# A long convolution rebuilt inside a two-phase kernel: phases by matmul, amplitudes by exponential, a 32x2 by 32 spectral split

## Chip, cores and metric

One core of a Trainium2 chip. The metric is device time in microseconds of one execution, the median of repeated runs. Engines are named as in the profile: PE (TensorE, matmul) and PEld (its weight loads), DVE (VectorE), ACT (ScalarE), POOL (GpSimd), SP (SyncE, here only a DMA queue).

## The reference, cut to what matters

Everything is float32, with L = 2048 positions, D = 512 channels, N = 128 modes per channel, F = 1792.

```python
x = A_u                                   # [1, 2048, 512]
h = x + conv(layernorm(x))
h2 = h + mixer(layernorm(h))

# conv
dt = exp(log_dt); A = -exp(log_A_real) + 1j*A_imag; C = (C_real + 1j*C_imag)*dt[:, None]
P = exp((A*dt[:, None])[:, :, None] * arange(L))        # [512, 128, 2048]
K = 2*einsum("dn,dnl->dl", C, P).real                   # the taps, [512, 2048]
y = irfft(rfft(u, 2L) * rfft(K, 2L))[:L] + u*D_skip     # along time, per channel

# mixer
h = gelu(layernorm(x) @ w1); four column groups shifted in time by +1, -1, +2, -2
x1 = x + shifted @ w2
out = x1 + gelu(layernorm(x1) @ w3) @ w4
```

Two parts are costly in the convolution: building the taps K, a sum of 128 damped oscillations for each channel and time, and the convolution itself, done by discrete Fourier transforms written as matmuls.

## The kernel before, in words

`tile_kernel` runs `conv_phase` and then `mixer_phase`. The residual `h` stays on chip, 16 blocks of 512 channels on 128 partitions.

**Taps.** Time l is split into a slow and a fast part, so that a tap is a product of two small tables summed over the modes. The modes lie on the 128 partitions. Channels go in 32 chunks of 16 (`CH`). For each chunk `table(g)` builds `cs` and `sn`, [128, 16 x 96] each: 64 columns per channel for one time factor (a lower half of 32 and an upper half of 32) and 32 for the other. A table entry is amplitude times cosine or sine of a phase. Phases are 32-bit integers that wrap once a turn: `params(t)` makes steps and starts for 128 channels, `steps` expands them on POOL into `p8` and `s8`, and `phases` adds them into `pt` on POOL, 1024 integers per partition and chunk. ACT takes sine of `pt` and, after an absolute value, cosine. Amplitudes are products of powers of the decay: `decay` makes powers in `E` by squaring on ACT, DVE multiplies them into the PSUM tile `amx` (in some chunks ACT squares part of them), and `amy` takes the second factor. Then DVE and POOL multiply: `snx` and `csx` on DVE (four operations of 512), `sny` and `csy` on one of the two by `SHARE`. `taps(s, g)` multiplies the tables on PE and ACT copies the result to `kt`.

**Spectra.** Channels go in four stages of 128 (`WID`). A transform of 32 times 64 points: `stage_a_taps` or `stage_a_turn` transforms `kt` over the first index with 32x32 tiles, and either ACT copies or DVE turns the result into `at`; `stage_a_x` does the same with the input. `stage_b` and `product` do the second index with `tbs` (128 rows, 64 columns a tile, eight products per `e`, eight `e` per stage), ACT copies one spectrum, DVE (or POOL, by `SHARE`) multiplies, and `stage_b_inv` goes back with `ms` (64 rows, 128 columns). `stage_a_inv` and `last_a_inv` finish with `fis` and add to `h`. There are two buffers `u` between product and inverse.

**Order.** Nearly every operation of `conv_phase` is a node of a planner (class `Plan`): engine, assumed cost, tiles that it reads and writes, and a nominal due time from `NOM`. The planner walks a model of the engines, the queues, the port that DVE and POOL share and the free PSUM banks (`grab`), and so fixes one order for each engine; `InOrder` then keeps it. Where PE would idle it inserts multiplications by the identity (`busy`). While stage s is transformed, the tables of stage s+1 are built, so the last stage has no tables beside it. PSUM has two banks' pairs, two single banks and `amx`. DMAs go out on the SP queue, except the first blocks of x on ACT's queue.

**Mixer.** Layers of split-precision (fp32r) matmuls on PE with GELU on ACT. It begins when the last quarter of `h` is there: statistics, normalisation (`norm_h`, `norm1`), `warm`, `layer1`.

All engine calls go through one recording helper, so nearly every instruction of the profile bears L88; rows are told apart by tile names.

Of the kernel before, what the change touches and what calls it, by code (L numbers as in the profile page):

```python
# [24 lines left out]
SHARE = {'mul0': [[1, 4], [0, 7]], 'mul2': [[6], []], 'amy': [[0, 1, 2, 3, 5, 6], [0, 1, 3, 4, 5, 6]], 'csy': [[5, 7], [0, 1, 2, 3, 4, 5, 7]], 'sny': [[1, 2, 4, 6, 7], [0, 1, 2, 4, 5, 6, 7]], 'sq': [[0, 1, 2, 3, 7], [1, 2, 3, 4, 6, 7]], 'turn': [[0, 1, 2, 4, 5, 6], [0, 2, 4, 6, 7]], 'hadd': [[0, 2, 6, 7], [1, 5, 6]], 'sum0': [[1, 5], [2, 4, 5]], 'sum1': [[], [2, 7]], 'sum2': [[2, 4, 6, 7], [1, 2, 4, 6, 7]], 'sum3': [[2, 3, 4, 5, 6, 7], [0, 2, 7]]}  # L25
# [8 lines left out]
PAIRS = 2  # L34
# [4 lines left out]
NOM = {'t0': 988.68, 'per': 120.18, 'ln': -591.43, 'kg0': -1777.07, 'kgs0': -98.74, 'kg': 84.04, 'kgs': 113.27, 'ak': 132.4, 'ax': -1187.75, 'b': -2.11, 'ib': 2.35, 'y': 1372.79, 'ys': 271.67, 'tr': -1417.89, 'exp': -7.85, 'wt': 1053.36, 'pr1': -308.92, 'pr2': 976.97, 'st': 1676.95, 'xa': 510.71, 'xs': -31.11}  # L39
TURN = 2.0 ** 32  # L40
TWO_PI = 2.0 * math.pi
SIN_SCALE = float(np.nextafter(np.float32(TWO_PI), np.float32(0))) / TURN
RAD = 683565248.0
# [3 lines left out]
def tables():  # L47
# [5 lines left out]
    a, b, k1, k2 = np.arange(32.0), np.arange(64.0), np.arange(32.0), np.arange(64.0)  # L53
    ph = 2 * np.pi * np.outer(a, k1 + 0.25) / 32
    fa = np.tile(np.stack([np.cos(ph), -np.sin(ph)], 1), (4, 1, 1)).astype(np.float32)
    fi = np.zeros((128, 2, 32), np.float32)
    for hi in range(2):
        fi[hi * 64 : hi * 64 + 64, hi] = np.concatenate([np.cos(ph), -np.sin(ph)], 1).T / L
    th = 2 * np.pi * b[:, None, None] * (k1[None, :, None] + 32 * k2[None, None, :] + 0.25) / L
    tb = np.zeros((128, 32, 128), np.float32)  # L60
    mm = np.zeros((128, 3, 16, 128), np.float32)
    for hi in range(2):
        c, s = np.cos(th[hi * 32 : hi * 32 + 32]), np.sin(th[hi * 32 : hi * 32 + 32])
        r, i = slice(hi * 64, hi * 64 + 32), slice(hi * 64 + 32, hi * 64 + 64)
        q = slice(hi * 32, hi * 32 + 32)
        tb[:64][q, :, :64], tb[:64][q, :, 64:] = c, -s
        tb[64:][q, :, :64], tb[64:][q, :, 64:] = s, c
# [1496 lines left out]
```

## Time and profile before

| | |
|---|---|
| runs | 723.45, 723.99, 725.02 us; median 723.99 |
| profiled execution, span | 723.0 us, 16573 instructions |
| PE busy / PEld | 672.0 us (93%) / 520.1 us (72%) |
| DVE | 536.4 us (74%) |
| ACT | 416.8 us (58%) |
| POOL | 394.9 us (55%) |
| first matmul of the mixer's warm-up | 321.66 us |
| mean granted PE clock | 0.983 |

The convolution fills the first 321.7 us, the mixer the rest. Busy shares over the span are means over these two; the windows by stage in the prediction tell them apart. PE's busy time holds identity multiplications that compute nothing.

### The profile page before, as it was taken

To read this page: it belongs to the slowest core of one execution; us is meant where nothing else is said; L and a number is where in the kernel's file an instruction comes from. 1 tells how busy PE (TensorE), PEld (TensorE's weight loads), DVE (VectorE), ACT (ScalarE), POOL (GpSimd) and SP (SyncE) were. 2 spreads that over 40 slices of the span, in tenths; PEclk is the share of its full clock that TensorE was granted. 3 is DMA by queue.
4 is the path that set the end of the run, shared out by engine and by line. 5 is a ranking of instruction groups with operands and counts; after the bars stand their busy time and mean duration, and the time that the engine had idled before them with its cause. 6 is when DMAs were issued, how large, how long until landed. Compare 5 with 4: busy or idle time off the path is not lost.

```text
span 723.0 us, 16573 instructions
## 1 busy us (share of the span) xinstructions
PE 672.0 (93%) x6812; PEld 520.1 (72%) x6812; DVE 536.4 (74%) x947; ACT 416.8 (58%) x724; POOL 394.9 (55%) x386
## 2 busy tenths in 40 slices
PE   3898499999999989989999999999999999999997
PEld 2887255754762765858888777888888888888886
DVE  3999999999789888988454789754667955545544
ACT  3897778866995887215646344575344644443430
POOL 0687389977997998302344334554345655534310
PEclk9999799999999999999999999999999999999999
DMA  8830053012000213020010002211111152111014
GB/s 229 231 129 16 2 161 76 2 47 77 16 17 24 39 38 98 2 60 0 1 30 29 1 0 59 59 44 44 48 40 60 51 159 81 45 44 58 1 30 117
DMA packets 42667, 40.98 MB, mean 57 GB/s; under 512 B 4704, under 2 KB 31328, under 8 KB 42592
## 3 DMA queue, kind: packets, MB, share of 16 engines
q1 hardware_dynamic: 41440, 37.83, 18.3%
q10 hardware_dynamic: 1152, 2.10, 1.2%
q8 instruction: 53, 0.87, 0.5%
q14 instruction: 22, 0.18, 0.1%
HBM read 33.62 MB, written 6.29 MB: 55 GB/s over the span
## 4 chain that ended last, share of the span: by engine, by line
PE 55%; DVE 21%; ACT 10%; POOL 7%; issue 4%; DMA 2%; SPq 1%; DVEq 0%; ACTq 0%; POOLq 0%
PE l L88 20%; PE acc L88 11%; ACT pt L88 6%; PE bank L88 6%; DVE u L88 4%; DVE at L88 3%; PE l3c L88 3%; PE l3d L88 2%; PE l3f L88 2%; PE l3g L88 2%; PE l3e L88 2%; PE l3a L88 2%; PE l3b L88 2%; DVE bs L88 2%; DVE cs L88 2%
## 5 line engine op out<-in xcount | busy, mean ns | idle before, releaser
L88 ACT ACTIVATE pt<-pt 128x1056 f32<-128x1056 int32 x64 | 70.0, 1094 | 20.6 <-DVE cs L88 8.6
L88 POOL TENSOR_TENSOR pt<-p,s 128x1024 int32<-128x1024 int32 x32 | 65.1, 2039 | 6.2 <-DVE sn L88 5.3
L88 PE MATMUL bank<-at,tbs 128*64 128x256 f32 (+1 forms) x640 | 63.3, 343 | 2.5 <-DVE at L88 1.2
L88 PE MATMUL bank<-ident 128*128 128x128 f32 x472 | 62.8, 288 | 0.0
L88 PEld LDWEIGHTS bank<-ident 128*128 128x128 f32 x472 | 58.0, 200 | 5.7 <-ACT E L88 1.7
L88 PEld LDWEIGHTS bank<-at,tbs 128*64 128x64 f32 x640 | 39.4, 135 | 22.4 <-DVE at L88 3.5
L88 PE MATMUL bank<-u,ms 64*128 64x128 f32 x736 | 50.9, 284 | 4.3 <-DVE u L88 1.8
L88 PEld LDWEIGHTS bank<-u,ms 64*128 64x128 f32 x736 | 44.5, 189 | 12.5 <-issue 4.6
L88 POOL TENSOR_TENSOR cs0w<-raw,cs0w 128x512 fp32r<-128x512 f32 x7 | 9.1, 1302 | 67.0 <-ACT cs0w L88 58.3
L88 DVE TENSOR_TENSOR cs<-pt,amx 128x512 f32<-128x512 f32 x64 | 41.0, 679 | 5.1 <-ACT amx L88 4.4
L88 DVE TENSOR_TENSOR h<-h,l 128x512 f32<-128x512 f32 x48 | 32.6, 686 | 14.9 <-PE l L88 14.8
L88 DVE TENSOR_TENSOR u<-u,l3f 128x512 f32<-128x512 f32 x14 | 9.6, 684 | 44.9 <-PE l3f L88 44.9
L88 POOL TENSOR_TENSOR cs1w<-raw,cs1w 128x512 fp32r<-128x512 f32 x7 | 9.1, 1298 | 61.4 <-ACT cs1w L88 61.4
L88 PE MATMUL bank<-cs 128*32 128x64 f32 x1024 | 32.9, 225 | 8.8 <-DVE cs L88 8.2
L88 PEld LDWEIGHTS bank<-cs 128*32 128x32 f32 x1024 | 24.1, 111 | 20.1 <-issue 14.8
L88 ACT ACTIVATE pt<-pt,halfpi 128x1056 f32<-128x1056 f32 x32 | 38.0, 1189 | 0.4
L88 DVE STREAM_TRANSPOSE at<-bank 128x512 f32<-128x512 f32 (+1 forms) x40 | 36.3, 933 | 1.6 <-PE bank L88 1.3
L88 ACT COPY at<-bank 128x512 f32<-128x512 f32 x40 | 25.2, 632 | 21.2 <-PE bank L88 21.1
L88 POOL TENSOR_TENSOR sn<-pt,amp 128x512 f32<-128x512 f32 x26 | 32.5, 1250 | 7.3 <-DVE amp L88 4.0
L88 ACT ACTIVATE u<-u 128x512 f32<-128x512 f32 x56 | 35.4, 633 | 1.8
L88 POOL TENSOR_TENSOR h<-h,x 128x512 f32<-128x512 f32 x16 | 22.0, 1384 | 24.7 <-DVE x L88 24.7
L88 PE MATMUL bank<-sn 128*32 128x64 f32 x1024 | 31.9, 223 | 2.6 <-DVE sn L88 2.1
(1156 smaller groups left out, 2118.4 us busy)
## 6 DMA issues: line engine op xcount, KB each, us to landing
raw<-in_B_w_dram SPq DMA_DIRECT2D x28, 256.0 KB, 2.7
h<-in_A_u_dram SPq DMA_DIRECT2D x16, 256.0 KB, 4.5
rawa<-in_B_w_dram SPq DMA_DIRECT2D x14, 256.0 KB, 2.9
rawb<-in_B_w_dram SPq DMA_DIRECT2D x14, 256.0 KB, 3.0
h<-in_A_u_dram SPq DMA_DIRECT2D x24, 128.0 KB, 3.5
ms<-in_mm_dram SPq DMA_DIRECT2D x4, 768.0 KB, 12.1
out_dram<-h SPq DMA_DIRECT2D x48, 64.0 KB, 1.7
tbs<-in_tb_dram SPq DMA_DIRECT2D x4, 512.0 KB, 7.5
```

The costliest lines, as they stand in the source:

```text
L88: ins = f(*args, **kw)
```

## The change

It rebuilds the tables and the transform's split and sets the order of the whole phase anew. The parts, in shortened diffs:

**Phases by matmul.** `params` now works for each 128 channels with modes across and channels down, splits three angles into a high and a low fp32r half (`moved`), and carries them through DRAM into the rows of a stationary matrix `S`, together with the decay rates (`lamf`). The moving operand `phs` (from a new input `ph`) holds the time steps, and a row that rounds to whole turns. `steps`, `p8`, `s8` and the integer phases go.

```diff
+        def out():
+            for d in R4:
+                add(name, 0.4, lambda d=d: queue(far_[:, :, d, :], hl[d : 128 : 4]), ...)
+        def rows(half):
+            src = far_[half * 16 : half * 16 + 16].rearrange("(g b) e d n -> b (e d) g n", b=2)
+            for b in range(2):
+                for c in range(2):
+                    r_ = b * 64 + 4 + c * 28
+                    add(name, 0.4, lambda b=b, r_=r_: queue(Sr[r_ : r_ + 24], src[b]), ...)
+        def stationary(half, early=False):
+            i = (2 * t + half) % 3
+            add("ACT", 0.96, lambda: act.copy(Ss[i], Sr), ...)
...
-        add("POOL", 1.91, phases, ...)
-        add("ACT", 0.97, lambda: act.activation(tc_, pi, AF.Abs), r=[kp], w=[kc])
-        add("ACT", 0.97, lambda: act.activation(pf, pi, AF.Sin, scale=SIN_SCALE), ...)
-        add("ACT", 1.07, lambda: act.activation(tc_, tc_, AF.Sin, scale=-SIN_SCALE, bias=halfpi), ...)
+        def phases(n, view):
+            for i in range(2):
+                pe.matmul(view[:, i, :], S[:, g % 4 * 2 + i, :], phs[:, n, :], start=True, stop=True)
+        p = add("PE", 0.45, lambda: phases(0, plan.view(p)), ..., bank=2)
+        c = add("PE", 0.45, lambda: phases(1, plan.view(c)), ..., bank=2)
+        add("ACT", 0.98, lambda: act.activation(whole(), whole(), AF.Sin, scale=SIN_SCALE), ...)
+        add("ACT", 0.98, lambda: act.activation(cosine..., plan.view(c), AF.Sin, scale=SIN_SCALE), ..., frees=c)
```

For block 0, `out` and `rows` go on ACT's queue, for the others on SP's. The sine is written in place, in PSUM.

**Amplitudes by exponential.** The 64 amplitudes of each channel come from ACT, from exponents made by matmul of the same `S`; every four chunks (`EB`) ACT changes to the exponential's table and back. `amx` goes, `E` shrinks to a third, `amy` stays.

```diff
-        add("DVE", 0.99, lambda: v.tensor_tensor(ax[:, :, :, 1:8], ...), r=[ek], w=["amx"])
...
+    def decays_of(gs):
+        add("ACT", 1.5, lambda: act.activation(tiny, halfpi, AF.Exp), w=["trig", "rate"])
+        for g in gs:
+            def exponents(g=g):
+                for i in range(2):
+                    pe.matmul(plan.view(ids[g])[:, i, :], Ss[g // 4 % 3][:, g % 4 * 2 + i, :], phs[:, 2, :], start=True, stop=True)
+            ids[g] = add("PE", 0.45, exponents, dense=0.3, ..., bank=2)
+            add("ACT", 0.98, lambda g=g: act.activation(..., plan.view(ids[g])..., AF.Exp), ..., frees=ids[g])
+        add("ACT", 1.45, lambda: act.activation(tiny, halfpi, AF.Sin), w=["rate", "trig"])
```

**Products of the tables.** Upper half and second factor now lie side by side, so that one operation of 1024 does both.

```diff
-        ... snx lower, snx upper, sny, csx lower, csx upper, csy: six operations of 512
+        add("DVE", dve(CH * 32), lambda: v.scalar_tensor_tensor(
+            sn[:, :, 0:32], sine()[:, :, 31::-1], -1.0, amp[:, :, 0:32], ALU.mult, ALU.mult), ...)
+        add("DVE", dve(2 * CH * 32), lambda: v.tensor_tensor(sn[:, :, 32:96], sine(), amp[:, :, 32:96], ALU.mult), ..., frees=p)
+        add(e1, c1_, lambda: eng1.tensor_tensor(cs[:, :, 0:32], tc_[:, :, 31::-1], amp[:, :, 0:32], ALU.mult), ...)
+        add(e2, c2, lambda: eng2.tensor_tensor(cs[:, :, 32:96], tc_, amp[:, :, 32:96], ALU.mult), ...)
```

**The transform.** Time's order on the partitions changes to 32x2 and 32. `tb` and `mm` are half as large. `stage_a_taps` goes: all taps take `stage_a_turn` (one node of eight matmuls, 32 rows and 128 columns, two pairs of banks). `stage_a_x` has two matmuls of 64 rows for eight, the last transforms two for four. `stage_b` has sixteen products per `e` on 64x32 tiles, `stage_b_inv` takes two `e` at a time on 32x64 tiles and two pairs of banks. There are four buffers `u`.

```diff
-                    pe.matmul(view[par * 64 : par * 64 + 64, o : o + w_], tbs[:, k, part * 64 : part * 64 + 64], src[:, :, k, :], ...)
+                    pe.matmul(view[quarter(par), q, ..., part, :], tbs[rows, k, part * 32 : part * 32 + 32], src[rows, ..., k, :], ...)
...
-                        pe.matmul(plan.view(p)[:, par, pair * w_ : pair * w_ + w_], ms[f, m, e * 2 + pair, :], q[f, t, pair, :], ...)
+                            pe.matmul(plan.view(p)[par // 2][q * 64 : q * 64 + 64, par % 2, i * w_ : i * w_ + w_],
+                                      ms[quarter(par), m, e0 + i, q, :], u_[i][quarter(par), t, q, :], ...)
```

**Shares, banks, order.** All eight banks are now four pairs, and a single-bank node takes a pair too.

```diff
-SHARE = {'mul0': [[1, 4], [0, 7]], 'mul2': [[6], []], 'amy': [[0, 1, 2, 3, 5, 6], [0, 1, 3, 4, 5, 6]], 'csy': ..., 'sny': ..., 'sq': ..., 'turn': [[0, 1, 2, 4, 5, 6], ...], 'hadd': [[0, 2, 6, 7], ...], 'sum0': [[1, 5], [2, 4, 5]], 'sum1': [[], [2, 7]], 'sum2': [[2, 4, 6, 7], [1, 2, 4, 6, 7]], 'sum3': [[2, 3, 4, 5, 6, 7], [0, 2, 7]]}
+SHARE = {'mul0': [[4, 7], [2, 3]], 'mul2': [[0, 3, 6, 7], [2, 3, 6]], 'amy': [[2, 3, 5, 7], [0, 1, 3, 4, 5, 7]], 'csl': [[1, 2, 3, 4, 6], [1, 2, 3, 7]], 'csu': [[3, 4, 6], [0, 1, 2, 3, 4, 5, 7]], 'hadd': [[2], ...], 'sum0': [[7], [0, 1, 2, 3]], 'sum1': [[0, 1], [6, 7]], 'sum2': [[3, 5, 7], [2, 4]], 'sum3': [[], [3, 4]]}
-PAIRS = 2
+PAIRS = 4
+NB, EB = 4, 4
-NOM = {'t0': 988.68, 'per': 120.18, ...}
+NOM = {'ak': 1184.65, 'ax': -934.91, ...}
```

For the tables (`amy`, `csl`, `csu`) the first list is for the chunks of the first 128 channels, the second for the rest, and names the chunks (modulo 8) that POOL takes; for `mul` the lists are two stages, for `sum` DVE and POOL.

In the mixer, the copies of `wrap` follow the new order of time (four per tile for three), and the input and output DMAs too.

More of the change, by code (lines that the diff above doesn't have):

```diff
@@ L722, in stage_a_turn @@
+        keys = [("a1", 2 * r + i, jp) for i in range(2) for jp in range(2)]
+        p = add("PE", 1.95, mm, dense=0.9, r=[("kt", r * 64 // CH + i) for i in range(64 // CH)] + ["fas"] + prm(s), w=keys, bank=4,
+                at=TS[s] - NOM["ak"] + 4 * r)
+        for jp in range(2):
             for i in range(2):
@@ L1044, in conv_phase @@
     rest = rates()
-    for t in range(4):
-        transpose(t)
     tables_of(0)
```

610 lines of the change are left out of this document (285 added, 325 removed).

## The prediction, as put on record before the result

> **What bounds the kernel now.** I read the page first (the span is 723.0 us), then the windows by stage, then the groups of instructions up to 321.7 us by engine, then the waits and single stretches of the timeline. The windows (start and end of a stretch, its length, then busy time and instructions of PE, PEld, DVE, ACT and POOL, granted clock, DMA share, GB/s):
>
> ```profile
> 0.00:11.10 11.10, 0.00 (x0) 0.00 (x0) 0.83 (x6) 1.98 (x3) 0.70 (x6) 1.00 0.79 205
> 31.30:280.00 248.70, 220.59 (x4301) 149.57 (x4299) 225.94 (x361) 199.29 (x356) 205.89 (x180) 0.96 0.19 56
> 280.00:321.70 41.70, 37.71 (x583) 26.48 (x583) 38.32 (x73) 13.28 (x22) 14.33 (x15) 1.00 0.13 41
> 321.70:723.00 401.30, 394.98 (x1790) 325.49 (x1790) 252.45 (x454) 184.79 (x314) 165.77 (x175) 0.99 0.16 46
> ...
> 0.00:321.70 321.70, 277.04 (x5023) 194.57 (x5023) 283.92 (x494) 232.04 (x410) 229.13 (x211) 0.97 0.25 69
> ```
>
> The convolution takes the first 321.7 us, the mixer the other 401.3. The mixer is TensorE back to back (395.0 of 401.3), and the change touches there only a few GpSimd copies and the order of rows in DMAs, so I cost it at nothing; its cover is GpSimd's idle 235 us, and without it 12 more copies, each under the 1.2 us of a 512-wide row below, would be 14 us at most. In the convolution VectorE is the fullest engine that does only useful work: 283.9 of 321.7, and of its 37.8 idle microseconds 10.3 are the first load. PE's 277.0 looks as full, but 62.8 of it is the first row below, mostly multiplications by the identity that keep the clock up:
>
> ```profile
> L88 PE MATMUL bank<-ident 128*128 128x128 f32 x472 | 62.8, 288 | 0.0
> DVE bs L88 <- DMA h<-in_A_u_dram: 10.2, 2, 9.2
> DVE amx L88 <- ACT amx L88: 6.4, 9, 1.1
> ```
>
> After the first load VectorE's largest wait is 6.4 us in nine pieces, as on the engine that all others are arranged around. So the stage is sized by VectorE's work, and I predict from its ledger.
>
> **VectorE.** Groups: operation, out<-in, shape, count, then busy us and mean ns of one.
>
> ```profile
> L88 DVE TENSOR_TENSOR cs<-pt,amx 128x512 f32<-128x512 f32 x64 | 41.0, 679 | 5.1 <-ACT amx L88 4.4
> L88 DVE TENSOR_TENSOR u<-xs,bank 128x1024 f32<-128x1024 f32 x21 | 25.5, 1216 | 5.8 <-ACT xs L88 5.3 <-PE bank L88 0.3
> L88 DVE SCALAR_TENSOR_TENSOR sn<-pt,amx 128x512 f32<-128x512 f32 x32 | 21.7, 678 | 0.0
> L88 DVE TENSOR_TENSOR sn<-pt,amx 128x512 f32<-128x512 f32 x32 | 21.6, 675 | 1.0 <-POOL u L88 0.7 <-ACT amx L88 0.4
> L88 DVE STREAM_TRANSPOSE at<-bank 128x512 f32<-128x512 f32 x24 | 16.3, 709 | 0.8 <-PE bank L88 0.7
> L88 DVE TENSOR_TENSOR amx<-E,amx 128x512 f32<-128x512 f32 x23 | 15.9, 690 | 5.8 <-ACT amx L88 4.6 <-issue 1.2
> L88 DVE TENSOR_TENSOR amx<-E,amx 128x896 f32<-128x896 f32 x9 | 9.8, 1087 | 1.9 <-ACT amx L88 1.9
> L88 DVE TENSOR_TENSOR cs<-pt,amp 128x512 f32<-128x512 f32 x9 | 8.2, 913 | 0.8 <-ACT pt L88 0.8
> L88 DVE TENSOR_TENSOR amp<-E,ec 128x512 f32<-128x512 f32 x8 | 6.3, 791 | 0.0
> L88 DVE TENSOR_TENSOR sn<-pt,amp 128x512 f32<-128x512 f32 x6 | 5.1, 850 | 0.5 <-ACT pt L88 0.5
> L88 DVE TENSOR_TENSOR u<-u 128x256 f32<-128x256 f32 x10 | 4.8, 518 | 0.1
> L88 DVE TENSOR_SCALAR s<-thp 128x256 int32<-128x256 int32 x8 | 4.1, 512 | 0.0
> L88 DVE TENSOR_SCALAR sh<-thp 128x256 int32<-128x256 int32 x8 | 2.6, 328 | 0.0
> L88 DVE TENSOR_TENSOR scratch<-scratch 128x128 f32<-128x128 f32 x10 | 2.5, 288 | 0.1
> ```
>
> Table work that goes: 41.0 + 21.7 + 21.6 + 15.9 + 9.8 + 8.2 + 6.3 + 5.1 and the integer shifts 4.1 + 2.6 = 136.3. What comes, for 32 chunks: the negated lower sine, 32 x 0.678 = 21.7; the upper sine times amplitude, 1024 wide with one input in PSUM, 32 x 1.216 = 38.9; by the new shares VectorE also has 15 lower cosines (15 x 0.79 = 11.9), 8 upper ones of double width (8 x 1.4 = 11.2, between 1.22 and twice 0.79) and 10 outer products (7.9). Sum 91.6, net -44.7. Elsewhere: two more blocks of taps are turned by VectorE, 8 x 0.709 = +5.7; six fewer spectral products (27 become 21) -7.3; one more pair of sums +1.0; two more additions into h at about 0.68, +1.4; low halves of the three parameters, 12 x 0.288, and one 512 wide, together +4.2; parameter blocks 2 and 3 apart instead of one of 256, some 20 more starts at about 0.1, +2. Net -37.7 by means. Means overlap a little: two that are 0.68 each end after 1.27 in the row of the timeline below, so I count 0.93 of it, **-35 us**.
>
> ```profile
> 258.71 1.27 DVE L88 TENSOR_TENSOR cs<-pt,amx 128x512 f32<-128x512 f32 x2
> L88 ACT ACTIVATE pt<-pt 128x1056 f32<-128x1056 int32 x64 | 70.0, 1094 | 20.6 <-DVE cs L88 8.6 <-POOL pt L88 8.4 <-POOL cs L88 2.2
> L88 ACT ACTIVATE pt<-pt,halfpi 128x1056 f32<-128x1056 f32 x32 | 38.0, 1189 | 0.4
> L88 ACT ACT_TABLE_LOAD x5 | 6.4, 1283 | 0.8 <-PEq L1551 0.7
> L88 POOL TENSOR_TENSOR pt<-p,s 128x1024 int32<-128x1024 int32 x32 | 65.1, 2039 | 6.2 <-DVE sn L88 5.3
> L88 POOL TENSOR_TENSOR sn<-pt,amp 128x512 f32<-128x512 f32 x26 | 32.5, 1250 | 7.3 <-DVE amp L88 4.0 <-ACT pt L88 3.2
> L88 POOL TENSOR_TENSOR cs<-pt,amp 128x512 f32<-128x512 f32 x23 | 27.6, 1200 | 5.5 <-ACT pt L88 5.3
> ```
>
> **Do the others follow?** GpSimd loses the phases (65.1), the sine share (32.5) and 23 cosines (27.6), and takes 17 lower and 24 double-width upper cosines, (17 + 48) x 1.2 = 78, and six products of two operations at about 1.4, 17: some -30, and less still with the small integer steps gone; it is no bound. ScalarE ran three passes of a chunk (absolute value, sine, cosine, 108.0) and runs three again (sine, cosine, exponential, 96 x 1.06 = 102). It gains about 9 casts of the stationary matrix at 1.1, and 16 table changes of 1.283 with a dummy of 0.2, +23.7; it loses the copies and squares of `amx`, two thirds of those of `E`, and eight copies of `at`, about 45. Net near -12, so 220 of some 287.
>
> TensorE gains six fp32r passes of 512 columns a chunk, 0.235 each by the mixer's 36 in 8.45, 45 us in all. In return its DFT goes to more, smaller tiles:
>
> ```profile
> 327.36 8.45 PE l L88 x36
> L88 PE MATMUL bank<-at,tbs 128*64 128x256 f32 x384 | 47.0, 389 | 1.8 <-ACT at L88 1.0 <-DVE at L88 0.5 <-DVE u L88 0.2
> L88 PE MATMUL bank<-u,ms 64*128 64x128 f32 x736 | 50.9, 284 | 4.3 <-DVE u L88 1.8 <-ACT at L88 0.7 <-issue 0.5
> L88 PE MATMUL bank<-kt,fas 32*32 32x512 f32 x192 | 11.2, 599 | 2.2 <-DVE kt L88 1.0 <-ACT at L88 0.9 <-DVE u L88 0.3
> 43.26 0.32 PE L88 MATMUL bank<-cs 128*32 128x64 f32 x8 [0.53 <-DVE mvh L88]
> 43.37 0.32 PE L88 MATMUL bank<-sn 128*32 128x64 f32 x8
> ```
>
> An fp32 product is two instructions, so 47.0 / 24 products = 1.96 us for 16 instructions; the new 32 on 64x32 tiles are eight abreast. The `kt,fas` row has 512 columns in 58 ns each where one alone takes 599, so ten overlap by their spans, and eight distinct tiles do run together. I take 1.1 us a product (27 ns an instruction, ends 0.85 and 1.96), nearest to that row, and half of 50.9 for the inverse. That is -20 and -25 against +45: TensorE is even, with filler in hand. It shortens each product's latency, which counts only in the last stage, below.
>
> The Trainium skill ("TensorE: Matmul & The Clock Gate", Part 1) says that starts of matmuls never come closer than about 25 ns. This trace differs: eight start from 43.26 to 43.37, 14 ns apart. By the page the inverse's 1536 instructions are an estimated 38 us instead of 25, which in the last stage alone would add some 4 us.
>
> **Last stage, 280.0 to 321.7.** VectorE is again 38.3 of 41.7 and loses three products and four pairs of sums; that is inside the 35, not added again. Bank turnover follows it.
>
> **The start.** This is what the change puts on the path. Parameters now go through DRAM: four stores, eight loads (of which four serve the first half), issued for block 0 on ScalarE's queue, and a cast, before the first phase matmul.
>
> ```profile
> 4.30 6.26 ACTq L88 DMA_DIRECT2D h<-in_A_u_dram  x6
> 21.66 0.22 DVE L88 TENSOR_SCALAR ini<-scratch 128x128 int32<-128x128 f32 x1
> 33.72 1.26 DVE L88 TENSOR_TENSOR cs<-pt,amx 128x512 f32<-128x512 f32 x2
> ...
> h<-in_A_u_dram SPq DMA_DIRECT2D x24, 128.0 KB, 3.5
> ms<-in_mm_dram SPq DMA_DIRECT2D x4, 768.0 KB, 12.1
> ```
>
> Angles are ready at 21.9 today; with one more operation, cast and subtraction, 22.9. Two hops at the 3.5 of a 128 KB load plus four issues each of 0.4 give 33; the cast, phase matmuls and sine (1.1 + 0.5 + 1.1) give 35.8, against 33.72 for the first table product now. The statistics of x and the next parameters cover part of VectorE's time. I take **+2 us**; with hops of 12.1, as for the bulk loads next to them, it would be +17, and at no less than 0 if all is covered.
>
> Sum: 723.0 - 35 + 2 = 690. The profiled span is 1.0 under the median of the runs, 723.99, so **691**.
>
> **Rivals.**
> 1. The start lands late: hops between 7 and 12.1 us give +9 to +17 instead of +2, 698 to 706, say 703. For it: the load share is 0.79 in the first window and six ACT-queue issues took 6.26 us. Against: ScalarE's ring is its own, and `tb` and `mm` are halved, so the bulk ends earlier.
> 2. ScalarE's exponential blocks starve VectorE: each holds the sine back for 1.5 + 4 x 1.06 + 1.5 = 7.2 us, eight times. If VectorE has nothing else for 2 us of each, +16: 707. Against: products and transposes are more than half of its work. Should the small tiles run only four abreast, TensorE is 45 fuller and the same range results.
> The Trainium skill ("ScalarE: Activation LUTs", What ACT_TABLE_LOAD costs) adds a drain of 1.38 us to each 1.283 load. This trace does not show it: idle time before all five loads is 0.8 us together, 0.7 of it at the program's start (row above). By the page 16 changes cost an estimated 22 us more of ScalarE, and this rival would be the likely one.
> 3. Slower than before: PSUM. The old kernel had four bank groups and `amx` apart; the new has four pairs, and a sine keeps its pair from the matmul until VectorE has read it twice. Pure work per chunk is 0.5 + 1.1 + 1.9 for the sine, 1.6 each for cosine and exponential, 1.3 for taps, 8.0 x 32 = 256 pair-us; products 32 x 2.9 = 93, inverse 16 x 2 x 2.3 = 74, taps' transform 8 x 2 x 4.8 = 77, the rest about 70: 570 over four pairs, 143 us. It decides where waiting stretches the mean hold over 2.26 times (321.7 x 4 / 570); at 2.4 the stage lasts 342 and the run 744. For it: hold times include the backlog of the fullest engine. Against: at a stage of 288 a stretch of 2.0 is still free.
> 4. The ledger shrinks and idle time with it (283.9 of 310.6 is kept as a ratio, and the start is covered): 675 or less.
>
> **How the numbers follow.** The forecast has 0.62, with its own range of 676 to 703 (6 either way on the shares of double width and tile rates, the start up to +9). Rival 1 has 0.14, rival 2 0.08, rival 3 0.10, rival 4 0.05, and 0.01 falls within 0.2% (1.4 us, about what a measurement here can tell). Faster 0.62 + 0.14 + 0.08 + 0.05 = 0.89; slower 0.10. Leaving out the slow case and half of rival 4, with a margin over rivals 1 and 2: 674 to 715.
>
> **What would show it.** After: VectorE near 249 busy before the mixer begins at about 289; group rows of 1024 at 1.2 us for the sine; 64x32 starts about 27 ns apart or less; table loads at 1.283 without a gap; first table product at 34 to 37. Wrong if the first phases wait past 42, if TensorE waits on releases of banks rather than on data, or if GpSimd's double-width cosines take well over 2.4 us and hold the table back.

## Result and profile after

The changed kernel takes 736.7 us (median of 732.6 to 738.5) against 724.5 for the kernel before: ratio 1.0161, 95% interval [1.0131, 1.0191], slower by 1.6%. On another chip it was 734.2 us, 1.0132 [1.0104, 1.0159]; below, its place is taken as the middle of the two, 1.0147. I had forecast 691. The profiled execution below was the quickest of the four, 732.6 us, 4 us under the middle.

The windows of the profiled execution (span 730.8 us), columns as before: the convolution, now to 329.65, and the mixer.

```profile
0.00:329.65 329.65, 242.72 (x5450) 149.89 (x5450) 263.81 (x431) 224.09 (x368) 168.53 (x136) 0.92 0.31 82
329.65:730.80 401.15, 394.87 (x1790) 326.69 (x1790) 253.24 (x454) 185.05 (x314) 169.69 (x187) 0.99 0.16 46
```

The mixer is what it was (401.15, before 401.30), so the whole difference is 8.0 us more of convolution. Yet in it every engine is busy for less time: PE 34, VectorE 20, ScalarE 8, POOL 61 us less. For PE that is not less work. Its identity multiplications fell by 44 us (62.8 before, row below), and all else that it does grew from 214 to 224 us. VectorE's idle time went from 37.8 to 65.8 us. The ledger was paid in part, and the time not at all.

Groups of instructions of the convolution after (operation, out<-in, shape, count, then busy us and mean ns, then idle time before):

```profile
L100 DVE TENSOR_TENSOR sn<-bank,amp 128x1024 f32<-128x1024 f32 x24 | 29.0, 1210 | 0.0
L100 DVE SCALAR_TENSOR_TENSOR sn<-bank,amp 128x512 f32<-128x512 f32 x24 | 16.4, 683 | 7.6 <-ACT bank L100 4.9 <-PE bank L100 1.7 <-issue 0.9
L100 DVE TENSOR_TENSOR cs<-pt,amp 128x512 f32<-128x512 f32 x11 | 13.4, 1218 | 0.0
L100 DVE TENSOR_TENSOR cs<-pt,amp 128x1024 f32<-128x1024 f32 x6 | 7.5, 1251 | 0.2 <-ACT pt L100 0.2
L100 DVE TENSOR_TENSOR amp<-E,ec 128x512 f32<-128x512 f32 x9 | 10.6, 1181 | 0.2
L100 DVE TENSOR_TENSOR u<-u 128x256 f32<-128x256 f32 x12 | 9.2, 809 | 1.3 <-POOL u L100 1.3
...
L100 ACT ACT_TABLE_LOAD x21 | 26.9, 1283 | 1.9 <-PEq L1531 0.7 <-DMA h<-in_A_u_dram 0.6 <-issue 0.2
...
L100 POOL TENSOR_TENSOR cs<-pt,amp 128x1024 f32<-128x1024 f32 x18 | 43.9, 2437 | 54.6 <-ACT pt L100 45.7 <-PE bank L100 8.7
...
L100 PE MATMUL bank<-phs,S 128*128 128x512 f32 x192 | 67.7, 467 | 28.4 <-ACT pt L100 10.1 <-DVE sn L100 6.0 <-ACT S L100 5.8
L100 PE MATMUL bank<-ident 128*128 128x128 f32 x126 | 18.6, 318 | 0.0
L100 PE MATMUL bank<-u,ms 32*64 32x128 f32 x1536 | 30.2, 277 | 7.7 <-issue 5.2 <-DVE u L100 0.8 <-ACT ec L100 0.5
L100 PE MATMUL bank<-at,tbs 64*32 64x256 f32 x768 | 24.9, 379 | 3.2 <-ACT pt L100 2.2 <-issue 0.6 <-DVE sn L100 0.4
```

The sine products cost what I priced (1.21 and 0.68 us), the table loads too (1.283, hardly a gap). What I priced too low are short operations with both inputs in SBUF: the lower cosines 1.22 instead of 0.79, the outer products 1.18 instead of 0.79, the sums 0.81 instead of 0.52. TensorE's new passes over `phs` are dearer too, 67.7 us and not 45. POOL, which was busy for 229 us before, now stands for 45.7 us waiting for ScalarE's cosines (`pt`).

Where is the time? I cut the convolution where ScalarE copies the eighth, sixteenth, ... chunk of taps, that is by blocks of 128 channels, first the kernel before, then the changed one:

```profile
0.00:84.00 84.00, 57.67 (x918) 53.57 (x926) 69.03 (x157) 63.53 (x115) 43.61 (x45) 0.96 0.45 131
84.00:156.30 72.30, 66.63 (x1198) 44.00 (x1191) 67.42 (x118) 56.97 (x106) 60.25 (x55) 0.96 0.25 71
156.30:220.00 63.70, 59.85 (x1281) 37.16 (x1268) 56.04 (x77) 51.04 (x90) 57.01 (x50) 0.97 0.12 32
220.00:281.60 61.60, 56.34 (x1128) 34.42 (x1132) 54.71 (x77) 47.84 (x81) 55.53 (x50) 0.97 0.17 41
281.60:321.65 40.05, 36.51 (x518) 25.37 (x519) 36.67 (x71) 12.66 (x20) 12.73 (x14) 1.00 0.14 42
```

```profile
0.00:84.70 84.70, 45.50 (x658) 34.69 (x658) 61.37 (x142) 62.16 (x101) 22.78 (x24) 0.86 0.51 138
84.70:156.10 71.40, 54.93 (x1265) 30.70 (x1265) 62.16 (x92) 53.62 (x95) 42.86 (x34) 0.93 0.32 91
156.10:222.60 66.50, 54.01 (x1297) 30.98 (x1296) 56.62 (x80) 48.15 (x80) 38.80 (x29) 0.95 0.20 50
222.60:283.90 61.30, 53.83 (x1269) 31.06 (x1269) 46.05 (x50) 45.95 (x71) 40.47 (x29) 0.97 0.22 53
283.90:329.65 45.75, 34.46 (x962) 22.46 (x962) 37.61 (x70) 14.21 (x25) 23.62 (x22) 0.92 0.19 52
```

Three things are to be seen. The first four blocks are as long as before (283.9 against 281.6 us) although VectorE lost 7.7 us in the first, 5.3 in the second and 8.7 in the fourth of them, and POOL a quarter to a half in each. And the last block is 5.7 us longer, with nearly twice as many matmuls. The third stands in the column of the granted clock: 0.97 over the whole convolution before, 0.92 after, and lower in four of the five blocks. It moves with the length of the second block. The same instructions took there, in the profiles of run `a_again` (the changed kernel once more) and `a_tail` (which differs only in the last block):

```profile
84.50:159.00 74.50, 56.25 (x1265) 31.32 (x1265) 62.17 (x91) 53.53 (x93) 42.17 (x34) 0.91 0.32 89
84.30:159.60 75.30, 57.40 (x1264) 32.61 (x1264) 61.22 (x89) 53.64 (x94) 42.15 (x34) 0.89 0.31 86
```

So 71.4, 74.5 and 75.3 us go with a clock of 0.93, 0.91 and 0.89. Which of the two follows the other these rows do not show, and no run holds the clock alone.

The first table product comes at 44.01, 10.3 later than before. Rows of the timeline (start, length, then engine and operation; in brackets the idle time before), first one of the kernel before, then the changed one:

```profile
11.14 0.19 ACT L88 ACTIVATE dts<-ldt 128x4 f32<-128x4 f32 x1
...
7.45 5.92 SPq L369 DMA_DIRECT2D dsk<-in_A_D_skip_dram  x4
...
12.73 0.32 ACTq L100 DMA_DIRECT2D h<-in_A_u_dram  x1
13.09 0.20 ACT L100 ACTIVATE dts<-ldt 128x4 f32<-128x4 f32 x1 [4.17 <-DMA aci<-in_A_C_real_dram]
...
34.05 1.04 ACT L100 CAST S<-Sr 128x1024 fp32r<-128x1024 f32 x1 [0.55 <-DMA Sr<-moved]
35.14 5.25 PE L100 MATMUL bank<-phs,S 128*128 128x512 f32 x14 [3.31 <-ACT S L100]
36.51 1.02 ACT L100 ACTIVATE amp<-bank 128x1024 f32<-128x1024 f32 x1
...
38.59 1.94 ACT L100 ACTIVATE amp<-bank 128x1024 f32<-128x1024 f32 x2
40.53 1.28 ACT L100 ACT_TABLE_LOAD   x1
...
41.93 1.01 ACT L100 ACTIVATE pt<-bank 128x1024 f32<-128x1024 f32 x1
44.01 1.19 DVE L100 TENSOR_TENSOR cs<-pt,amp 128x1024 f32<-128x1024 f32 x1
```

The exponential of dt, on which every parameter waits, stands in ScalarE's order behind a load of x that ScalarE itself issues, and that load was issued only at 12.73. But in the kernel before the exponential ran hardly earlier, at 11.14, so this makes 2 of the 10.3 us. The way through DRAM was as long as I had it: the cast of the stationary matrix starts at 34.05, the first phase matmul at 35.14. Most of what is late comes behind it. ScalarE first makes the exponentials of four chunks and changes its table back, from 36.51 to 41.93, and only then the first cosine.

### The profile page after: what moved, and what is told of

Same layout as the page of the kernel before. It is cut to its first block, busy times and chain, and to the rows that moved or that the text cites. A ratio compares the mean times of both kernels' runs of the same rounds, so it can differ in the third digit from the quotient of the medians.

```text
span 730.8 us, 17385 instructions
## 1 busy us (share of the span) xinstructions
PE 637.6 (87%) x7240; PEld 476.6 (65%) x7240; DVE 517.1 (71%) x884; ACT 409.1 (56%) x682; POOL 338.2 (46%) x323
## 4 chain that ended last, share of the span: by engine, by line
PE 54%; DVE 8%; issue 2%; ACT 1%; POOL 0%; ACTq 0%; DVEq 0%
PE l L100 19%; PE acc L100 10%; PE bank L100 5%; PE l3c L100 2%; PE l3d L100 2%; PE l3f L100 2%; PE l3g L100 2%; PE l3e L100 2%; PE l3a L100 2%; PE l3b L100 2%; DVE at L100 1%; DVE u L100 1%; PE xt L100 1%; PE x1t L100 1%; DVE x L100 1%
## 5 line engine op out<-in xcount | busy, mean ns | idle before, releaser
L100 PE MATMUL bank<-phs,S 128*128 128x512 f32 x192 | 67.7, 467 | 28.4 <-ACT pt L100 10.1
L100 POOL TENSOR_TENSOR cs<-pt,amp 128x1024 f32<-128x1024 f32 (+1 forms) x31 | 62.0, 2018 | 55.0 <-ACT pt L100 46.0
L100 PEld LDWEIGHTS bank<-phs,S 128*128 128x128 f32 x192 | 34.3, 208 | 55.7 <-ACT pt L100 15.7
L100 DVE STREAM_TRANSPOSE at<-bank 128x512 f32<-128x512 f32 (+1 forms) x48 | 39.0, 863 | 11.3 <-PE bank L100 11.1
L100 ACT ACTIVATE pt<-bank 128x1024 f32<-128x1024 f32 x40 | 41.0, 1024 | 7.1 <-POOL cs L100 3.8
L100 DVE TENSOR_TENSOR h<-h,l 128x512 f32<-128x512 f32 x48 | 32.6, 686 | 14.8 <-PE l L100 14.7
L100 PE MATMUL bank<-at,tbs 64*32 64x256 f32 (+1 forms) x1280 | 35.8, 343 | 6.9 <-DVE at L100 2.3
L100 PEld LDWEIGHTS bank<-cs 128*32 128x32 f32 x1024 | 25.9, 118 | 22.3 <-issue 10.3
L100 POOL TENSOR_TENSOR cs0w<-raw,cs0w 128x512 fp32r<-128x512 f32 x7 | 9.1, 1304 | 65.1 <-ACT cs0w L100 57.0
L100 PE MATMUL bank<-u,ms 32*64 32x128 f32 x1536 | 30.2, 277 | 7.7 <-issue 5.2
L100 ACT ACTIVATE bank<-bank 128x1024 f32<-128x1024 f32 x32 | 32.0, 1013 | 5.3 <-PE bank L100 5.2
L100 PEld LDWEIGHTS bank<-u,ms 32*64 32x64 f32 x1536 | 24.2, 130 | 15.3 <-issue 8.9
L100 PEld LDWEIGHTS bank<-at,tbs 64*32 64x32 f32 x1280 | 20.7, 107 | 20.2 <-ACT pt L100 3.8
L100 DVE TENSOR_TENSOR sn<-bank,amp 128x1024 f32<-128x1024 f32 x24 | 29.0, 1210 | 0.0
```

Source lines behind the costliest of these rows:

```text
L100: ins = f(*args, **kw)
```

## Experiments

Where "order kept" is said, each engine's order of instructions is the one that the planner made for the parent kernel. Changes in us are against the parent: ratio differences times 724.8.

**1. Is the stage sized by VectorE's work?** My forecast turned VectorE's ledger into time almost one to one. So I took 32 products of 512 out of VectorE, in either kernel, order kept; the columns that they make stay zero.

```diff
-        add("DVE", dve(CH * 32), lambda: v.scalar_tensor_tensor(sn..., -1.0, ...), ...)   # snx in the kernel before
+        add("DVE", dve(CH * 32), lambda: None, ...)
```

> The kernel before without its 32 negated sine products (32 x 0.678 = 21.7 us of VectorE, all in the convolution; their half of the sine table stays zero). The order of everything else is kept. Theory V (VectorE's work sizes the convolution, as the prediction took it): the time falls by 17 to 21 us, to about 704. Theory C (a chain of hand-offs between engines, kept in a fixed order, sizes it, and VectorE is only the fullest link): it falls by well under half of that, 3 to 9 us.

Measured: 721.9 us, 0.9958 [0.9926, 0.9989]. 21.7 us of VectorE's work were worth 3.0, by the interval 0.8 to 5.4.

> The changed kernel without its 32 negated sine products (32 x 0.682 = 21.8 us of VectorE; that part of the sine table stays zero), order kept. Theory V: 17 to 21 us less, about 717. Theory C: VectorE already stands idle 44 us after its first table product, so it falls by 0 to 8 us.

Measured: 727.2, 1.0031 [1.0007, 1.0055], 8.4 us less. The premise of the forecast falls here: VectorE is the fullest engine of both kernels, and its work is worth 0.14 us each in the one and 0.39 in the other. The profile of the kernel before says the same in another way. It follows the convolution back from its last instruction and gives the shares of that chain by tile (releasers are inferred):

```profile
by line: ACT pt L88 13.2%; PE bank L88 12.6%; issue 8.2%; DVE u L88 6.9%; DVE at L88 6.5%; DVE bs L88 5.1%; DVE cs L88 4.7%; DVE scratch L88 4.0%; POOL pt L88 3.9%; POOL u L88 3.7%; DVE sn L88 3.2%; DMA h<-in_A_u_dram 2.5%; POOL cs L88 2.4%
```

VectorE's tiles are some 30% of it, and the sine table, from which the products were taken, 3.2%.

**2. The other engines.** ScalarE without the table switches (the exponentials become copies of the same size), order kept; and, in the kernel before, POOL without its 32 phase sums (ScalarE reads a constant in their place), order kept.

> The changed kernel without changes of ScalarE's function table for the amplitudes: the 32 exponentials are plain copies of the exponents and the 16 dummy activations go (the amplitudes are then not computed). Order kept, 16 x 1.48 = 23.7 us of ScalarE less. Theory T (the exponential blocks hold the sines back, and that stretches the chain): 10 to 24 us less. Theory C with VectorE and PSUM as its links: 2 to 8 us less. Theory V: nothing, VectorE's work is the same.

Measured: 728.0, 1.0037 [1.0007, 1.0067]: 7.9 us for 23.7 of ScalarE.

> The kernel before, order kept, without POOL's 32 phase sums (65.1 us; ScalarE's sines and absolute values read a constant instead). My prediction priced POOL's relief at nothing by itself, since VectorE held the stage. Theory J (the order is fixed, relief of one engine alone is worth a tenth to a third of it): 3 to 12 us faster, 712 to 722. Rival N (POOL's work had slack everywhere): within 2 us of the kernel before.

Measured: 721.5, 0.9945 [0.9926, 0.9964]: 4.0 us for 65.1 of POOL, 0.06 each. POOL's relief, the largest of the change, had almost no price of its own.

Both reliefs of the changed kernel together:

> The changed kernel, order kept, without the 32 negated sine products of VectorE (-21.8 us) and without the 16 switches of ScalarE's table (-23.7 us; the exponentials become copies of the same size): what a_less_dve and a_no_tables left out, together. Theory J (with the order of each engine fixed, the chain passes from engine to engine, and work taken from one engine alone is replaced on the chain by another's): the two together give more than the sum of the two alone. Alone they gave some 9 us each against the changed kernel's first median, 4 to 6 by their spans; together 18 us or more, 712 to 719, and the five blocks' ends come earlier from the second block on. A replay of the two fixed orders with the durations of the trace gives -3.3 and -3.6 alone and -11.5 together. Rival A (both lie on one chain, one after the other): exactly the sum. Rival B (something else paces both, such as loads or the supply of instructions): less than the larger of the two, 727 or more.

Measured: 722.8, 0.9971 [0.9948, 0.9994], 11.7 us less than the changed kernel on the same chip. Alone they gave 8.4 and 7.9, so together less than their sum and more than the larger: theory J, as I had put it in medians, falls; the plain sum, rival A, is 4.6 us off, hardly outside the scatter. (By the mixer's start in single profiles it looks the other way, 4.5 and 3.9 alone against 11.3; these scatter by 2 us, 329.65 and 331.9 for the changed kernel.) What holds is the size: 45 us of work off two engines move the end by 12.

```profile
0.00:318.30 318.30, 236.28 (x5450) 147.78 (x5450) 247.62 (x399) 201.17 (x336) 172.48 (x138) 0.94 0.32 85
```

VectorE is busy 247.6 here, what I had forecast for the changed kernel (249), and ScalarE 19 us under my figure for it; the mixer begins at 318, not at 289.

**3. PSUM pairs.** Rival 3 of the prediction. The sines of every second chunk go to a tile in SBUF, which frees their pair some 2 us earlier, order kept.

```diff
-        act.activation(whole(), whole(), AF.Sin, scale=SIN_SCALE)
+        act.activation(to(), whole(), AF.Sin, scale=SIN_SCALE)      # to(): tile "even" where g is even
```

> The changed kernel, order kept, with the sines of every second chunk written to a tile in SBUF instead of back into their pair of banks; the pair can be refilled when ScalarE has read it, about 2 us earlier. Rival 3 of the prediction (the pairs held by the sines size the stage): the TensorE stretches that end on a release by the sine products (14.8 us in all) shrink by about half and the time falls by 5 us or more. Theory O (the fixed order with its late start and late partners sizes it): within 2 us of 736.7, or longer by up to 5 us, because the 1024-wide sine product now reads two SBUF operands and meets POOL's double-width cosines.

Measured: 746.3, 1.0297 [1.0246, 1.0348], 11 us longer. TensorE's waits for sine products went from 14.8 to 11.3 us, less than the half that the rival asked, and the end came later, by more than either theory gave. VectorE's rows, first the sines from SBUF, then those still in PSUM:

```profile
L100 DVE TENSOR_TENSOR sn<-even,amp 128x1024 f32<-128x1024 f32 x16 | 25.9, 1620 | 0.0
L100 DVE TENSOR_TENSOR sn<-bank,amp 128x1024 f32<-128x1024 f32 x8 | 9.7, 1212 | 0.0
```

The same operation takes 1.62 us on average with two inputs in SBUF and 1.21 with one in PSUM. The Trainium skill (SBUF — State Buffer, "SBUF: two separate sides") says that VectorE with two SBUF inputs and GpSimd lock a shared pair of ports for a whole instruction, and that the other waits. These rows agree, and so do the three short groups above that came out too long. So does a group that did not: VectorE's own double-width cosines, also with both inputs in SBUF, took 1.25 us, in chunks in which POOL makes no product of that kind. The negated sine products from SBUF grew as well, from 0.68 to 1.17. Nothing speaks for rival 3 here, but the run does not rule it out, since VectorE's busy time rose by 14 us (263.8 to 278.0), and that can hide what the earlier release gave.

**4. POOL's long operations.** If such locks size the stage, shorter ones help: each double-width cosine product on POOL as two of 512, order kept.

> The changed kernel, order kept; each of POOL's cosine products over 64 columns (2.44 us, 24 of them) is written as two over 32 columns (about 1.2 us each). If VectorE's lost time (24.0 us over the shortest of each form, 17.5 before) comes from standing behind POOL's long operations and this sizes the stage, an operation of VectorE waits at most 1.2 us instead of 2.4: VectorE's excess falls by 5 us or more and the time by 3 to 8 us. Theory O: VectorE's excess may fall, the time stays within 3 us of 736.7.

Measured: 735.3, 1.0156 [1.0132, 1.0179]: no change. VectorE's busy time fell by some 3 us to 260.7, and two of the short groups did shrink,

```profile
L100 DVE TENSOR_TENSOR cs<-pt,amp 128x512 f32<-128x512 f32 x11 | 11.3, 1031 | 0.0
L100 DVE TENSOR_TENSOR u<-u 128x256 f32<-128x256 f32 x12 | 8.0, 704 | 1.4 <-POOL u L100 1.3
```

and the time did not follow. That is not enough to clear the locks: 3 us at the 0.39 of run 1 would be 1.2 us, less than these runs can tell, and 14 us more of VectorE's time in a_sine_sbuf went with 11 us more in all. The locks explain most of what VectorE's term of the sum missed; how much of the time they hold stays open.

**5. The start.** Once without block 0's way through DRAM (its rows are loaded from x, so that they need not wait for the store), order kept; once with x's first loads on SP's queue, planned anew.

> The changed kernel without the stores of block 0's angles to DRAM: its loads into the stationary rows read rows of the input x instead and wait for nothing (the tables of the first 128 channels are then wrong). Order kept. Theory S (the late start is passed on in full to the end): the store and its wait took 23.01 to 28.70 us, so the first table product comes 3 to 6 us earlier and the whole is 3 to 6 us shorter. Rival (the start is late because the first loads and ScalarE's blocked queue are late, or slack later absorbs it): under 2 us.

Measured: 735.1, 1.0137 [1.011, 1.0165], no change; its first table product is at 44.26. The store is not priced by this: the loads that stand in for the rows were issued 2.2 us earlier (26.54 for 28.70) but took longer, so that the cast behind them starts at 33.83 and not 34.05.

> The changed kernel with the first eight loads of x taken from ScalarE's queue and put on SyncE's; the order is planned anew. Theory S (8 of the 12.7 us come from the first loads: ScalarE stands behind its own queue until 13.09): the exponential of dt is done by 9 to 10, the first table product by 39 to 41 instead of 44.0, and the end 3 to 5 us earlier, 731 to 734. Theory O: the start comes earlier, but the newly planned order is another draw, planned at 300.7 instead of 293.4 us, so that the total is 736 to 748.

Measured: 731.8, 1.0105 [1.008, 1.0131], 3.0 us less. Timeline of ScalarE, VectorE and TensorE in it:

```profile
4.18 0.19 ACT L100 ACTIVATE dts<-ldt 128x4 f32<-128x4 f32 x1
...
36.48 1.79 DVE L100 TENSOR_TENSOR cs<-pt,amp 128x1024 f32<-128x1024 f32 x2
...
80.30 2.25 PE L100 MATMUL bank<-h,fas 64*128 64x512 f32 x4 [4.08 <-ACT h L100]
```

The exponential of dt runs at 4.18 instead of 13.09, the first table product comes 7.5 us earlier, more than theory S asked. But the first block ends at 84.5, as before (84.7): TensorE stands there 4.08 us for normalised rows of x, whose transform the new order puts in front of the block's last taps (in the changed kernel it begins at 91.04). So an earlier start and a new order together are worth about 3 us; the run does not part them.

**6. The last block.** In runs of small matmuls TensorE stands still with no semaphore on the instruction that follows ("issue"). Its timeline in the changed kernel:

```profile
307.27 0.91 PE L100 MATMUL bank<-u,ms 32*64 32x128 f32 x39 [1.08 <-issue]
308.11 1.16 PE L100 MATMUL bank<-at,tbs 64*32 64x128 f32 x64
309.20 0.78 PE L100 MATMUL bank<-u,ms 32*64 32x128 f32 x25
311.11 2.08 PE L100 MATMUL bank<-u,ms 32*64 32x128 f32 x128 [1.14 <-issue]
314.84 1.35 PE L100 MATMUL bank<-u,ms 32*64 32x128 f32 x71 [1.65 <-issue]
```

Between two such stops lie exactly 128 matmuls (39 + 64 + 25, then 128) and their 128 weight loads, 3.84 and 3.73 us from start to start. The three stops are 3.9 us together. The Trainium skill (Runtime: NRT & Kernel Launch, "Instruction fetch mechanics") says that engines get their instructions in blocks of 256 and that the change of block is mostly hidden. The count agrees with this trace; hidden it is not, where 256 instructions run in 2.1 to 2.7 us. That the stops are this change of block is argued from the count; the trace does not name them. I left out half of the matmuls of the last block's six products with four terms, order kept.

```diff
-                for n, (m, t) in enumerate(terms[i]):
+                used = terms[i] if s < NS - 1 else terms[i][:2]
+                for n, (m, t) in enumerate(used):
```

> The changed kernel, order kept; in the last block of 128 channels the six inverse products with four terms compute two of them (half of their matmuls left out). Theory T (the last block is 45.7 us long from its last tap copy to the mixer instead of 40.0, because TensorE, in runs of 32x64 matmuls, stands for 1.3 to 2.0 us after each 128 of them with no semaphore to wait for, 4.6 us in all): the standstills at 307, 311 and 315 us vanish and the end comes 3.5 to 5.5 us earlier. Rival P (the last block is set by POOL's three products and VectorE's sums): less than 1.5 us.

Measured: 731.5, 1.0081 [1.0045, 1.0117], 3.7 us less than the changed kernel beside it, and the last block is 40.5 us long (288.1 to 328.6).

```profile
311.01 0.42 PE L100 MATMUL bank<-at,tbs 64*32 64x128 f32 x7 [0.37 <-issue]
...
312.95 2.06 PE L100 MATMUL bank<-u,ms 32*64 32x128 f32 x64 [0.38 <-POOL u L100]
```

The stops shrink to 0.4 and the block to the length of before. That is theory T's size, though 3.7 us has some 3 us either way by the two intervals. A low clock is not needed for the longer block: in a_order1 (below) it is 45.2 us at a granted clock of 1.00. (TensorE's work in the block is smaller too, by 192 matmuls, 3.8 us at the group's 20 ns, so the run alone doesn't part supply from work. What speaks for supply is the stops themselves: they wait for no semaphore, come at every 128th matmul, and all but vanish. In a_order1 to a_order3 and a_cal the block is 43 to 46 us with most or all of its matmuls.)

The base of runs 2 (both) and 6, on their chip:

> The changed kernel itself once more, as the base that shares its chip with the next two: 733 to 738, the mixer's start at 329 to 334.

Measured: 734.2, 1.0132 [1.0104, 1.0159], the mixer at 331.9.

**7. The order.** The planner fixes every engine's order from assumed costs. For the changed kernel it put the convolution's end at 293.4; the chip took 329.7. Among the costs that are off by the trace: parameter steps with two inputs on VectorE 0.20 planned and 0.44 spent, loads 2.2 us to landing planned and 3.5 spent by the 128 KB row of the kernel before, the four loads of `dsk` 0.3 and 1.48 (5.92 for four, above). First, such costs corrected, with the old due times `NOM`:

```diff
-    SEM = {..., "SP": 2.2, "AQ": 2.2}
+    SEM = {..., "SP": 3.0, "AQ": 3.0}
-        one, two, acts = 0.07 + N * 0.53e-3, 0.07 + N * 1.045e-3, 0.11 + N * 0.833e-3
+        one, two, acts = 0.15 + N * 0.53e-3, 0.17 + N * 1.045e-3, 0.15 + N * 0.833e-3
...
-XQ = 2
+XQ = 0
```

> As a_xq0, and with the planner's costs set to what the trace of the changed kernel measured: VectorE's parameter steps 0.09 us longer, its complex sums 0.6, loads 3.0 us to landing instead of 2.2, the four loads of D_skip 1.3 us each and later, the two phase tables 2.5 and 1.7 us. The arithmetic is the same; only the order changes. The planner puts the end of the convolution at 322 us (293 with its own costs, 329.7 measured). Theory O (the order is made for costs that the chip doesn't have): the end comes near the plan, 320 to 327, so 722 to 732 in all, and the distance from plan to trace shrinks from 36 us to under 10. Rival (the new chain of dependencies itself is that long, whatever the order): 734 to 742, since nothing was taken out.

Measured: 732.1, 1.0109 [1.0086, 1.0132], mixer at 330.3. The plan came nearer, 8 us off instead of 36, but the time is that of a_xq0 (731.8), which has the same queue for x and the old costs: costs alone gave nothing. The due times had been fitted to the old ones. So the due times were fitted anew to the new ones (VectorE's sums at their unlocked 0.7 us); `a_order2` also holds the planner to 0.03 us for each small matmul.

> The arithmetic of the changed kernel, with a_cal's measured costs in the planner, and its due times tuned again against these costs (planned end of the convolution 311.6 instead of 322.1). Theory O (the order holds the time): as the plan for a_cal was met to 8 us (322.1 planned, 330.3 measured), the mixer starts at 317 to 323 and the time is 719 to 726. Rival D (dependencies and engines hold it, whatever the order): 729 to 736 like a_cal.

> As a_order1, with TensorE's supply of instructions in the planner as well (a run of small matmuls takes at least 0.03 us for each), planned end 321.1, where the same planner puts a_cal's due times at 336.5. Theory O: no later than a_order1 by more than 3 us, mixer at 316 to 322, 717 to 726. Rival D: 729 to 736.

Measured: 723.5, 0.9979 [0.9956, 1.0001], and 722.2, 0.9958 [0.9936, 0.998], mixer at 319.5 and 318.8. The same arithmetic, 12 and 14 us faster than the changed kernel and 9 and 11 faster than a_cal, whose queue for x they share; a_order2 is also faster than the kernel before. Theory D falls, and theory O's times came. What is not shown is the road. The granted clock of the convolution is 0.96 and 0.95 here for 0.93 in a_cal, and the second block, where most of the gain lies against the changed kernel (60.5 and 62.4 us for 71.4), has 1.00 and 0.97 for 0.93. Whether the order gains by itself or through the clock no run tells. Nor was a second search made with the old costs, which might also have found a better order.

Last, the sums of three products of the last block on VectorE, which leaves 96 small matmuls out, and the same care for the kernel before:

> The arithmetic of the changed kernel, order planned as for a_order2 (measured costs, TensorE's supply of instructions), with the sums of three products of the last block on VectorE, which halves their inverse matmuls; planned end 317.3 instead of 321.1. Theory T: the last block shrinks by 2 to 4 us and the time is 717 to 722. Rival: the last block keeps its 45 us (VectorE takes over as its limit), 721 to 727.

Measured: 719.3, 0.9896 [0.9872, 0.9921], the fastest of all, 1.0% under the kernel before. Its blocks, in the same columns:

```profile
0.00:79.50 79.50, 43.53 (x658) 32.67 (x660) 62.72 (x149) 64.22 (x107) 23.49 (x25) 0.88 0.54 153
79.50:141.20 61.70, 51.93 (x1266) 28.93 (x1264) 53.88 (x79) 50.31 (x89) 38.79 (x33) 0.99 0.36 98
141.20:207.70 66.50, 52.01 (x1297) 29.84 (x1295) 57.54 (x86) 48.01 (x79) 39.74 (x30) 1.00 0.21 50
207.70:271.30 63.60, 55.96 (x1269) 31.86 (x1269) 43.93 (x52) 45.30 (x71) 41.75 (x30) 0.95 0.22 51
271.30:317.66 46.36, 35.69 (x882) 24.74 (x882) 39.69 (x76) 14.20 (x25) 23.66 (x21) 0.88 0.18 51
```

and a row of TensorE's timeline in its last block:

```profile
300.50 2.02 PE L100 MATMUL bank<-u,ms 32*64 32x128 f32 x64 [2.03 <-DVE u L100]
```

The total is in theory T's range, the reason is not: the last block kept its 46 us, as the rival had it, and TensorE now waits there for VectorE (last row). Against the changed kernel the gain lies in the first two blocks, 5 and 10 us.

> The arithmetic of the kernel before, with the planner's costs set to its trace in the same way (loads 3.0 us, parameter steps 0.1 longer, phase sums 2.0) and its due times tuned anew, x's first loads on SyncE's queue; planned end 318.1 where the same planner puts the old due times at 328.4 to 330.9 (321.7 measured). Theory G (the change frees engine time that a good order can use): the kernel before gains less than the changed one did by its new order (14 us) and stays above a_order2: 718 to 727. Rival E (the order is all, the change nothing): 708 to 716, as far below before as a_order2 lies below the changed kernel.

Measured: 728.9, 1.0046 [1.0024, 1.0068], 3 us slower than before, where theory E had it at 708 to 716. Planned at 318.1, it ended at 327.9. And the corrected planner had its old order at 328.4 to 330.9, where the chip took 321.7: it misjudges by 7 to 10 us, and which way differs. So a fit to measured costs is no recipe by itself. Theory G is borne out as far as this: the changed kernel gained by the treatment, the kernel before did not. A longer search for it might end otherwise.

## Why the prediction was wrong, by its own steps

- **"The stage is sized by VectorE's work"** is the step that failed. I took 283.9 of 321.7 us busy for a bound, and small waits for its sign. The runs price VectorE's work at 0.14 us a microsecond in that kernel, not 0.93. Here an engine that is 88% full, while others of a fixed order are 71 to 86% full, was not the bound; by its shares (run 1) the chain to the end changes engines.
- **VectorE's term**, -35 by ledger, measured -20 (263.8 busy instead of 249): 15 us short. The three short groups that stand beside POOL's cosines make 11.5 of it (lower cosines 4.6, outer products 3.5, sums 3.4), and the parameter steps, some 12 us more than before where I had 6, most of the rest. At the measured price, 0.14, the 20 us that did go would be worth 3.
- **TensorE, "even, with filler in hand"**: its work without the identity multiplications grew by 10 us. The products and the inverse shrank as I had it, but the `phs` passes took 67.7 us, not 45: 0.35 each, where I took 0.235 from the mixer. The filler was spent (62.8 to 18.6 us), and the granted clock fell from 0.97 to 0.92, which is in no term and no rival of mine.
- **POOL -30, ScalarE -12, "no bound"**: measured -61 and -8. (ScalarE's items in my sum add to -18; I left the 6 us of its three passes out.) I priced POOL's relief at nothing by itself; b_less_pool says 0.06 each. That was right. At the runs' prices the change's reliefs add up to 0.14 x 20 + 0.06 x 61 + 0.33 x 8 = 9 us.
- **The start, +2**, first table product at 35.8: it came at 44.0. The hops were right to 1 us, the first phase matmul came at 35.1 (my mark of 42 was for that). What I left out is the four exponentials and the change of table that stand before the first cosine, 5.4 us on ScalarE; rival 2 has this block, but not on this path. That the lateness was worth little (first block 84.7 us long, 84.0 before) I had not foreseen.
- **Last stage, "inside the 35, not added again"**: +5.7 us. I set the inverse at half of 50.9 and the products at 27 ns an instruction. Products came out at 32 ns by their group (24.9 for 768), the inverse at 30.2 busy for 1536, both near. Not in the sum were TensorE's stops after each 128, 3.9 us. The Trainium skill's 25 ns (TensorE: Matmul & The Clock Gate, Part 1), by which I had put an estimated 4 us on this stage and set it aside, comes nearer to the loss than my own figure, by luck: the group ran at 20 ns, under that floor, and what the trace shows is stops.
- **Rivals.** 1 (start, +9 to +17) had the first table product late, 10.3 us after the kernel before, but not by slow hops, and the lateness was absorbed. 2 (exponential blocks starve VectorE): the table loads have no gap; without switches the kernel gains 7.9 us, so they cost half of the 16 that I gave. 3, the only one on the right side, got no support from a_sine_sbuf, and a_order1 and a_order2 with the same four pairs end 10 us earlier, so the pairs alone do not hold the time; it is not ruled out as a part. 4's 675 does not come out of its own ratio, which gives 686. An order that could be bettered by 9 to 11 us with the same arithmetic was not among them, nor was the clock.
- **The mixer at nothing**: right, 401.15 against 401.30.

So the 41 us between the forecast of the mixer's start (289) and 329.65 are, roughly, since the prices come from two kernels and carry their intervals: 26 that the reliefs were not worth (35 less 9), 5.7 in the last block, 1 more from the start than the 2 I gave (a_xq0's 3), and some 8 that are left. a_order2 begins the mixer 10.8 us earlier than the changed kernel with the same arithmetic, which is about the start and these 8 together. That another order removes them is shown; that the costs in the plan put them there is not, and neither is how much of it went through the clock or the locks. Which wait of the first four blocks each of them was is not settled, and neither is whether the last block's stops can go with all its work done.

## What to carry to other kernels

Where every engine keeps a fixed order, do not take the occupancy of the fullest one for a bound: price a relief by a run that takes work out with the order kept. In these two kernels it was worth 0.06 to 0.39 of the work. Where an order is planned, compare plan and trace and search for the order again before judging the arithmetic; here that moved the changed kernel by more than the change itself had, though the same care left the kernel before 3 us slower. When a path grows, walk it to its end: the first result waits for everything that stands in front of it on each engine. Look at the clock column too, and count instructions as well as work: halving a tile may double what the engine must be fed.

## What was not expected of the hardware

- TensorE stopped for 1.1 to 1.7 us after each 128 matmuls with their weight loads, where these ran in 2.1 to 2.7 us, 3.7 and 3.8 us from stop to stop. In `a_again`, `a_no_hop`, `a_cal` and `a_xq0`, which keep the count, the stops are 0.5 to 1.9 and the distances 3.3 to 4.0 us.
- The same VectorE product took 1.21 us with an input in PSUM and 1.62 on average with both in SBUF beside a busy POOL.
- A load that ScalarE issues held up ScalarE's own next instruction: the exponential of dt, which waited 4.2 us and ran at 13.09, ran at 4.18 when SyncE issued the loads.
- The same instructions took 71.4 to 75.3 us in one block, with a granted clock of 0.93 to 0.89.
